# Chunks 0 to 5 of a gated linear attention: outputs as quadrant products, V in one transfer, and a new order of the work

## The chip, the cores and the metric

One core of a Trainium2 chip. The metric is device time in microseconds (us), the median of several executions. Engine names as in the profile: PE (TensorE matmuls) and PEld (its weight loads), DVE (VectorE), ACT (ScalarE), POOL (GpSimd), SP (SyncE, which issues nearly all DMAs).

## The reference

A gated linear attention and, on its output, a feed-forward network (FFN). Inputs q, k, v, alpha have shape (4, 8, 768, 48): batches, heads, steps, head size.

```python
for t in range(S):
    state = alpha[:, :, t, :, None] * state + np.einsum('bhd,bhe->bhde', k[:, :, t], v[:, :, t])
    y[:, :, t] = np.einsum('bhd,bhde->bhe', q[:, :, t], state)
...
x = attn_out.transpose(0, 2, 1, 3).reshape(B * S, H * D)      # 3072 x 384
h = x @ w_in                                                   # 384 x 2048
g = np.where(h >= 1, h, np.where(h <= -1, 0.0, (h + 1) ** 2 / 4))
return (g @ w_out).astype(np.float32)                          # 2048 x 384
```

The weights arrive as 64-bit floats and are decoded on the chip.

## The kernel before

**Chunks.** The 3072 steps are cut into 24 chunks of 128 (`CH`), six to a batch. Heads are taken in four pairs (`G`); a pair's two heads lie on partitions 0 to 47 and 64 to 111. For each chunk `prepare` loads a (alpha), k, q and v, and DVE runs two scans: products of alpha forwards into `Q` (L563), then backwards, inverted, into `inv` (L587). `Q` is multiplied by q (L613) and `inv` by k (L603). Early chunks get a, k or q with steps on the partitions (`tok_`), so PE first transposes them, four transposes to a tensor ("flips", L502); later ones get them laid by head dimension (`dim_`). Before, a and k are flipped for chunks 0 to 6 and q for chunks 0 and 1 (`EARLYQ`).

**Attention of a chunk** (`attend`, `follow`). A chunk has two halves of 64 steps. PE transposes the keys (L677), makes the scores of both halves (L690, 16 products in quadrants of the array), and the halves' updates of the state (L703). The scores are masked by DVE (L773) or, for one of the two heads in chunks 0 to 4, copied by ACT (L745) and masked by POOL (L755). The outputs (L827) are products over 128 partitions: one stationary tile `both` holds V on 64 partitions and the state on the other 64, and the moving tiles `Q` and `other` hold masked scores on one half and Q on the other. That needs copies: the state into `both` (L719, L720), half of `Q` into `other` (L737), and V twice, as `vt` and as `both` (L524, L535). The output goes to `ring` as a rounded part (ACT, L851) and its remainder (DVE, L856).

**FFN.** Three chunks form a group (`GROUP`), 16 column blocks f of w_in and w_out each. A group's block is 9 products with w_in (L924), the nonlinearity (ACT L953 twice, DVE L967, ACT L973, and a remainder by DVE or POOL, L974), and 9 products with w_out (L995). Groups 0 and 1 take blocks 0 to 7 first and 8 to 15 later, so that fewer weights are needed at the start. A block of group 0 with f = 0 is split by chunk (`SPLIT`), as 9 products of 128 columns. Two blocks share a weight unit u, each with a w_in and a w_out tile, decoded in six steps: ACT L380 and L388, DVE L396 and L407, POOL L420, ACT L433, then the remainder L435 on POOL or DVE.

**What sets the order.** Every operation is an entry with an engine, a duration and a due time (`key`), and `Plan.order` turns these into one fixed program order for each engine; engines and SP run their rows strictly in that order. Where the plan expects PE to wait over 0.45 us, and a PSUM bank is free, it puts in products of zeros (`fill`, L1084). Constants and tables at the file's top (`SHIFT`, `PREP`, `WFETCH`, ...) move due times of single chunks and weight units.

## Time and profile before

| | us |
|---|---|
| median of 3 runs | 505.77 (504.51 to 505.97) |
| profiled execution, its time | 505.32 |
| its span, first to last instruction | 503.6 |
| outside the span | 1.7 |
| PE busy in the span | 491.6 |
| DVE / ACT / POOL busy | 306.0 / 307.6 / 225.8 |

PE is busy for 98% of the span, but "busy" counts the products of zeros too, and the time of 4817 products is the sum over stages that differ: about 65 us in which chunks are prepared, weights are loaded and decoded and PE is partly filled, then some 430 us in which FFN products follow each other without a gap. Rows of the timeline carry: start, duration of the row's first to last instruction, engine, line, operation, tiles, shapes, count, and in brackets the idle time before and what ended it. An fp32 product of 64 rows or columns shows as two instructions.

### The profile page before, as it was taken

The page shows a single profiled execution, that of the slowest core. Times are in us where ns is not written, and L with a number is a line of the kernel's source. Part 1 is how long each engine was busy: PE and PEld are TensorE (multiplying, and loading weights), DVE is VectorE, ACT ScalarE, POOL GpSimd, SP SyncE. Part 2 cuts the span into 40 slices and gives each one's busy share as a digit, 9 for nine tenths or more (in the row PEclk, how much of TensorE's full clock was granted, in tenths as well). Part 3 has the DMA queues.
Part 4 walks back from the last instruction along what each step waited for, and adds up shares of the span by engine and source line. Part 5 has one row for each costly group of instructions (what it writes and reads, how often), then busy time and mean ns, then how long its engine had stood idle before and what let it go on. Part 6 is the DMA issues. An engine that isn't in the chain of part 4 may idle for free.

```text
span 503.6 us, 12167 instructions
## 1 busy us (share of the span) xinstructions
PE 491.6 (98%) x4817; PEld 475.4 (94%) x4817; DVE 306.0 (61%) x588; ACT 307.6 (61%) x599; POOL 225.8 (45%) x256
## 2 busy tenths in 40 slices
PE   7998999999999999999999999999999999999995
PEld 5887899999999999999999999999999999999995
DVE  6899988988957538866457457457457513121112
ACT  2689999968553656565555655556555655555551
POOL 4588564344245434545445534445355332333330
PEclk9999999999999999999999999999999999999998
DMA  8999978012345535455244443343213300000001
GB/s 226 358 262 321 351 246 235 9 53 64 112 112 166 147 75 134 116 156 153 51 113 113 115 105 107 74 117 101 65 34 62 90 0 13 14 17 31 1 1 51
DMA packets 61886, 57.56 MB, mean 114 GB/s; under 512 B 35745, under 2 KB 47617, under 8 KB 61825
## 3 DMA queue, kind: packets, MB, share of 16 engines
q1 hardware_dynamic: 61680, 56.64, 39.7%
q8 instruction: 39, 0.64, 0.5%
q14 instruction: 23, 0.18, 0.1%
q10 hardware_dynamic: 144, 0.10, 0.1%
HBM read 44.83 MB, written 9.83 MB: 109 GB/s over the span
## 4 chain that ended last, share of the span: by engine, by line
PE 89%; DMA 4%; DVE 2%; ACT 2%; SPq 1%; issue 1%; DVEq 0%
PE ps L924 40%; PE ps L995 39%; PE ps L827 5%; DMA raw<-in_laid_tok_k 2%; PE ps L703 2%; PE ps L690 2%; DMA vt<-in_laid_v 1%; PE ps L1084 1%; PE ps L502 1%; DMA ring<-ring 1%; SPq L485 1%; ACT gf L953 0%; PE ps L677 0%; SPq L872 0%; DVE Q L773 0%
## 5 line engine op out<-in xcount | busy, mean ns | idle before, releaser
L924 PE MATMUL ps<-ring,wt 128*128 128x384 f32 (+1 forms) x1170 | 223.6, 337 | 1.3 <-DMA ring<-ring 0.5
L995 PE MATMUL ps<-wt,gh 128*128 128x384 f32 x1152 | 222.5, 339 | 0.0
L924 PEld LDWEIGHTS ps<-ring,wt 128*128 128x128 f32 x1170 | 204.3, 188 | 2.4 <-DMA ring<-ring 0.9
L995 PEld LDWEIGHTS ps<-wt,gh 128*128 128x128 f32 x1152 | 201.2, 188 | 1.2
L974 POOL TENSOR_TENSOR gh<-gf,gh 128x384 fp32r<-128x384 f32 x101 | 108.9, 1080 | 171.0 <-ACT gh L973 167.8
L967 DVE SCALAR_TENSOR_TENSOR gf<-gf,ps 128x384 f32<-128x384 f32 x102 | 56.1, 550 | 149.7 <-ACT gf L953 148.4
L953 ACT ACTIVATE gf<-ps,half_b 128x384 f32<-128x384 f32 (+1 forms) x130 | 74.9, 577 | 92.7 <-PE ps L924 90.9
L973 ACT CAST gh<-gf 128x384 fp32r<-128x384 f32 x102 | 52.3, 513 | 63.0 <-DVE gf L967 63.0
L953 ACT ACTIVATE gf<-gf 128x384 f32<-128x384 f32 (+1 forms) x130 | 67.6, 520 | 3.9
L420 POOL TENSOR_TENSOR w<-w,wt 128x768 int32<-128x768 int32 x16 | 31.3, 1959 | 34.2 <-issue 7.7
L613 POOL TENSOR_TENSOR Q<-Q,raw 128x512 f32<-128x512 f32 x23 | 30.0, 1304 | 6.2 <-DVE bwd L567 3.8
L804 POOL TENSOR_TENSOR state<-state,last 128x192 f32<-128x192 f32 x20 | 18.6, 928 | 29.1 <-DVE state L729 28.1
L773 DVE TENSOR_TENSOR Q<-ps,mask 64x256 f32<-64x256 f32 x48 | 20.3, 422 | 15.1 <-ACT other L737 13.3
L827 PE MATMUL ps<-other,both 128*64 128x64 f32 x372 | 26.8, 225 | 0.0
L827 PE MATMUL ps<-Q,both 128*64 128x64 f32 x372 | 26.8, 225 | 0.0
L827 PEld LDWEIGHTS ps<-Q,both 128*64 128x64 f32 x372 | 23.5, 138 | 2.8 <-issue 1.3
L587 DVE TENSOR_TENSOR_SCAN inv<-raw,bwd 128x511 f32<-128x511 f32 x17 | 23.5, 1383 | 0.0
L827 PEld LDWEIGHTS ps<-other,both 128*64 128x64 f32 x372 | 23.5, 138 | 0.0
L563 DVE TENSOR_TENSOR_SCAN Q<-raw,fwd 128x512 f32<-128x512 f32 x17 | 20.7, 1219 | 0.2
L719 ACT COPY both<-state 48x192 f32<-48x192 f32 x49 | 17.1, 349 | 1.5 <-DVE state L727 0.5
L856 DVE TENSOR_TENSOR ring<-ps,ring 128x512 fp32r<-128x512 f32 (+1 forms) x24 | 16.1, 672 | 3.1 <-ACT ring L851 2.6
L703 PEld LDWEIGHTS ps<-vt,ks 64*64 64x64 f32 x352 | 13.4, 135 | 4.8 <-issue 3.5
(81 smaller groups left out, 473.9 us busy)
## 6 DMA issues: line engine op xcount, KB each, us to landing
both<-in_laid_v_both SPq DMA_DIRECT2D x48, 128.0 KB, 3.6
wt<-in_laid_w_in SPq DMA_DIRECT2D x8, 768.0 KB, 8.1
wt<-in_laid_w_out SPq DMA_DIRECT2D x8, 768.0 KB, 7.7
raw<-in_laid_dim_q SPq DMA_DIRECT2D x22, 256.0 KB, 2.8
out<-ot SPq DMA_DIRECT2D x23, 192.0 KB, 2.1
raw<-in_laid_dim_a SPq DMA_DIRECT2D x17, 256.0 KB, 2.9
raw<-in_laid_dim_k SPq DMA_DIRECT2D x17, 256.0 KB, 2.9
blocks<-part SPq DMA_DIRECT2D x15, 256.0 KB, 2.0
```

Of the source, the lines that this page charges most:

```text
L420: add = lambda e, c=c: e.tensor_tensor(out=bits()[:, c], in0=bits()[:, c], in1=word(I32, 0)[:, c], op=ALU.add)
L563: lambda: nc.vector.tensor_tensor_scan(flat(Q()), aT(), flat(fwd), 0.0, ALU.mult, ALU.max),
L587: lambda: nc.vector.tensor_tensor_scan(flat(inv())[:, 0:n][:, ::-1], aT()[:, 1 : n + 1][:, ::-1], flat(bwd)[:, 0:n][:, ::-1], bwd[:, G - 1 ...
L613: mul = lambda e: e.tensor_tensor(out=flat(Q()), in0=flat(Q()), in1=qT(), op=ALU.mult)
L703: nc.tensor.matmul(out=up(j, u)[64 * r : 64 * r + 64, g], lhsT=turnt[j]()[halves[u], g, 64 * r : 64 * r + 64], rhs=V[j]()[halves[u], g] if ...
L827: nc.tensor.matmul(out=ps()[halves[r], to, halves[u]], lhsT=lhsT[:, r, u], rhs=x()[:, g, halves[u]], start=m + u == 0, stop=True, skip_gro ...
L924: nc.tensor.matmul(out=h(), lhsT=win(f, w)[:, kt], rhs=ring[:, at, kt, a, :], start=(m == 0), stop=(m == 3 * KT - 1),)
L953: lambda: nc.scalar.activation(out=gf(), in_=in_(), func=func, scale=scale, bias=bias),
L967: lambda: nc.vector.scalar_tensor_tensor(out=x(), in0=gf(), scalar=1.0, in1=h(), op0=ALU.min, op1=ALU.max),
L973: plan.op("ACT", 0.08 + (0.45 if x is h else 0.41) * w, key + 0.4, lambda: nc.scalar.copy(out=gh()[:, 0], in_=x()), [x], [gh])
L974: sub = lambda e: e.tensor_tensor(out=gh()[:, 1], in0=x(), in1=gh()[:, 0].bitcast(F32), op=ALU.subtract)
L995: nc.tensor.matmul(out=o_ps[seg][t](), lhsT=gh()[:, a, (t - c0) * CH : (t - c0 + 1) * CH], rhs=wout(f, w), start=(f == f0 and i == 0), sto ...
```

## The change

Constants: `J0 = 6` makes chunks 0 to 5 (j < `J0`) take the new path; `EARLYQ` goes from 2 to 6 (q is flipped by PE for chunks 0 to 5); `KHELP = 2` and `QHELP = 2` let ACT copy k and q of chunks 0 and 1 out of PSUM and POOL multiply; `KPOOL = 9` gives POOL the multiplication by k of chunks 7 and 8; `ALONE` from 2 to 5 lets POOL or DVE, instead of DVE alone, take the remainder (L435) of units 2 to 4. The other constants and all tables of due times have new numbers, and the plan counts DMA time in packets.

For chunks 0 to 5:

- V arrives once, as one transfer of 192 KB (`tok_v`), in place of one of 96 KB and two of 128 KB.
- The outputs are separate products in quadrants: masked scores with V (64 rows) and Q with the state (48 rows). State and Q are no longer copied; the state before and after each half is kept in a ring of four tiles (`snap`), and the masked scores are one tile `other` of 128 partitions.
- The first part of the values' products ("crossed", r = 1 - u) stands ahead of the state's update on PE, the rest behind it.
- For each head one mask operation of 128 partitions takes the place of two of 64.

For later chunks `both` is packed, 48 columns to a head in place of 64, so V's two transfers are 96 KB each. The zeroing of `both` (L286) moves from the start to a place behind chunk 3's masks on POOL.

```diff
-EARLYQ = 2
+EARLYQ = 6
...
-ALONE = 2
+ALONE = 5
...
+J0 = 6
+SNAPS = 4
+NV = 2
+MEETN = 2
+KHELP = 2
+KPOOL = 9
...
+            if j < J0:
+                V[j] = lambda: vts[:, j % NV]
+                plan.op(
+                    "SP",
+                    Plan.ISSUE,
+                    key - LOAD + 1,
+                    lambda: nc.sync.dma_start(out=V[j]()[:, 0:DM], in_=laid["tok_v"][j]),
...
+            by_k = lambda e: e.tensor_tensor(out=flat(inv()), in0=flat(inv()), in1=kT(), op=ALU.mult)
+            if j < KHELP:
+                kq = buf("stage", "raw", [P, G * CH], 8)
+                plan.op("ACT", 0.55, key + 0.2, lambda kT=kT: nc.scalar.copy(out=kq(), in_=kT()), [kt], [kq])
+                kt, kT = kq, lambda: kq()
+            if EARLYK <= j < KPOOL or j < KHELP:
+                plan.op("POOL", 1.3, key, lambda: by_k(nc.gpsimd), [inv, kt], [inv], port=True)
...
+        def mask_apart(j, key):
+            S = others[j]
+            for r in range(2):
+                if j < (HELP if r else HELP0):
...
+                plan.op(
+                    "DVE",
+                    0.45,
+                    key,
+                    lambda r=r: nc.vector.tensor_tensor(
+                        out=S()[:, r], in0=ss(j, r), in1=mask[:, None].broadcast_to([P, G, HC]), op=ALU.mult
+                    ),
...
+        def rest_of(j, u, key, reads):
+            if group_of[j]:
+                return
...
+            plan.op("POOL", 0.3, key, lambda: nc.gpsimd.tensor_copy(out=to, in_=src()), reads, [name], port=True)
...
+        def outputs_apart(j, ps):
+            Q, S, n = prepared[j][0], others[j], group_of[j]
+            heads = [(g, g) for g in range(KT if n == 0 else G)]
...
+            def values(crossed):
+                ways = [(kt, KT, rest_v[:, :, kt]) for kt in range(KT) if n == 0] + [(g, g, None) for g, _ in heads]
+                for i, (to, g, v_) in enumerate(ways):
+                    for u in range(2):
+                        r = 1 - u if crossed else u
+                        lhsT = vs(j, u, r, g, wide) if v_ is None else v_[halves[u], r]
+                        put(to, r, u, lhsT, S()[halves[u], r, g], crossed and i == 0)
+
+            def states():
...
+                    for u in (1, 0)
+                    if snaps[j, u] is not None
+                    for to, g, s_ in ways
+                    for r in range(2)
...
+            def others_():
+                first_, *more = states()
+                first_()
+                values(False)
+                for x in more:
+                    x()
+            return lambda: values(True), others_
...
+                if j < J0:
+                    mask_apart(j, key)
+                    rest_of(j, None, key, [vt])
...
+                    crossed, rest = outputs_apart(j, lambda: ps())
+                    reads = [others[j], vt, *(["rest_v"] if n0 else [])]
+                    o = plan.op("PE", 0.05 + pair * (2 * KT if n0 else G), key, crossed, reads, [ps], mode="quad")
+                plan.op("PE", 0.55, key + 0.02, lambda: update(j), [ks, *v_of], meets[j], mode="quad", beside=True, after=[o])
+            if j < J0:
+                follow_apart(j, key)
+                us = 0.05 + pair * (2 * KT if n0 else G) * (3 if j % PER else 2)
+                plan.op("PE", us, key + 0.1, rest, [*used(j), *(["rest_v"] if n0 else [])], [ps], mode="quad")
+                end_chunk(j, ps, key + 0.1)
```

The numbers of PE's instructions in the whole program: products of zeros 105 before and 43 after, flips 64 and 80, output products 408 (L827) and 516 (288 at L1031, 228 at L909); key transposes, scores, updates and FFN products are as many as before.

How the order changes shows at three places. In after's program the flips are L528, the key transposes L738, the scores L751, the updates L771, the new products L909, FFN products L1146 and L1217.

**PE at chunk 0's attention.** Before, chunk 1's flips, then chunk 0's keys, scores and updates:

```order
L502 MATMUL ps<-ident,raw 128x128 x12
L677 MATMUL ps<-ident,inv 128x128 x4
L690 MATMUL ps<-Q,inv 64x64 x16
L703 MATMUL ps<-vt,ks 64x48
L703 MATMUL ps<-both,ks 64x48 x2
...
L502 MATMUL ps<-ident,raw 128x128 x8
```

After, from chunk 0's keys on:

```order
L738 MATMUL ps<-ident,inv 128x128 x4
L751 MATMUL ps<-Q,inv 64x64 x16
L528 MATMUL ps<-ident,raw 128x128 x12
L909 MATMUL ps<-other,both 64x64 x6
L909 MATMUL ps<-other,vt 48x64 x6
L771 MATMUL ps<-vt,ks 64x48 x16
L738 MATMUL ps<-ident,inv 128x128 x4
L751 MATMUL ps<-Q,inv 64x64 x16
L909 MATMUL ps<-Q,snap 48x64
```

Chunk 2's flips (all of a, k and q) and 12 crossed products now stand between chunk 0's scores and its updates, and chunk 1's keys and scores ahead of the rest of chunk 0's outputs.

**SP's transfers from chunk 2 on.** Before (tok_a, tok_k and dim_q are a, k and q; wt a weight tile):

```order
L485 DMA raw<-in_laid_tok_a 128x464
L485 DMA raw<-in_laid_tok_k 128x464
L485 DMA raw<-in_laid_dim_q 128x512
L535 DMA both<-in_laid_v_both 64x512 x2
L459 DMA wt<-in_laid_w_in 128x768
L524 DMA vt<-in_laid_v 128x192
L459 DMA wt<-in_laid_w_out 128x768
L485 DMA raw<-in_laid_tok_a 128x464
L485 DMA raw<-in_laid_tok_k 128x464
```

After, chunk 1's V, then chunk 2's a, k and q:

```order
L551 DMA vt<-in_laid_tok_v 128x384 x2
L511 DMA raw<-in_laid_tok_a 128x464
L511 DMA raw<-in_laid_tok_k 128x464
L511 DMA raw<-in_laid_tok_q 128x464
L485 DMA wt<-in_laid_w_in 128x768
L485 DMA wt<-in_laid_w_out 128x768
L485 DMA wt<-in_laid_w_in 128x768
L485 DMA wt<-in_laid_w_out 128x768
L511 DMA raw<-in_laid_tok_a 128x464
```

Ahead of chunk 3's a there were two weight tiles; now there are four.

**PE from chunk 6's keys to its scores.** Before, from chunk 6's keys (products of zeros, and chunk 5's outputs L827, are in the lines left out):

```order
L677 MATMUL ps<-ident,inv 128x128 x4
...
L924 MATMUL ps<-ring,wt 128x384 x9
...
L690 MATMUL ps<-Q,inv 64x64 x16
...
L924 MATMUL ps<-ring,wt 128x384 x18
```

After, the same stretch:

```order
L738 MATMUL ps<-ident,inv 128x128 x4
...
L909 MATMUL ps<-other,vt 64x64 x8
L771 MATMUL ps<-vt,ks 64x48 x8
L1146 MATMUL ps<-ring,wt 128x384 x9
L909 MATMUL ps<-Q,snap 48x64
L909 MATMUL ps<-other,vt 64x64 x8
L909 MATMUL ps<-Q,snap 48x64 x15
L1146 MATMUL ps<-ring,wt 128x384 x18
L751 MATMUL ps<-Q,inv 64x64 x16
```

Up to the end of chunk 6's scores and updates PE has 81 FFN products in its row before (63 at L924, 18 at L995) and 117 after (81 and 36); all attention of chunks 0 to 5 lies ahead of that point in both. From there on FFN products follow each other in both, broken only by the later chunks' bursts.

## Rows read from the trace of the kernel before

**Rows 1.** Stretches of 20 us: length, busy us by engine, granted clock, DMA share, GB/s
```profile
0.00:20.00 20.00, 16.59 (x256) 13.39 (x257) 14.84 (x33) 7.75 (x17) 9.33 (x24) 1.00 0.92 267
20.00:40.00 20.00, 19.46 (x356) 16.92 (x356) 18.54 (x42) 17.10 (x36) 16.45 (x21) 1.00 0.97 299
40.00:60.00 20.00, 18.29 (x263) 16.50 (x260) 19.05 (x43) 19.32 (x40) 13.11 (x13) 1.00 1.02 341
```

**Rows 2.** Timeline of PE: the FFN products behind chunk 6's scores and updates
```profile
62.13 3.40 PE L924 MATMUL ps<-ring,wt 128*128 128x384 f32 x18 [0.36 <-DVE ring L856]
```

**Rows 3.** Chain that ended last, by time: start, us, engine, line, count
```profile
33.75 1.96 PE ps L924 x18
...
114.36 3.14 PE ps L924 x18
```

**Rows 4.** Timeline of PE: products of zeros, at the start and later
```profile
1.06 3.38 PE L1084 MATMUL ps<-zeros 128*128 128x256 bf16 x15 [1.06 <-DVE zeros L259]
...
14.58 1.80 PE L1084 MATMUL ps<-zeros 128*128 128x256 bf16 x15
```

**Rows 5.** Timeline of PE: bursts of chunks 0, 1, 4
```profile
16.75 0.27 PE L827 MATMUL ps<-Q,both 128*64 128x64 f32 x1
...
18.29 0.70 PE L690 MATMUL ps<-Q,inv 48*64 48x64 f32 x32
...
21.55 1.19 PE L502 MATMUL ps<-ident,raw 128*128 128x128 f32 x8
22.67 0.27 PE L827 MATMUL ps<-Q,both 128*64 128x64 f32 x1
...
40.47 0.69 PE L690 MATMUL ps<-Q,inv 48*64 48x64 f32 x32
40.98 0.20 PE L703 MATMUL ps<-vt,ks 64*64 64x48 f32 x1
```

**Rows 6.** Timeline of DVE: preparation of chunk 1
```profile
9.40 0.16 DVE L553 TENSOR_SCALAR fwd<-ps 128x4 f32<-128x4 f32 x1
...
11.28 1.27 DVE L587 TENSOR_TENSOR_SCAN inv<-ps,bwd 128x511 f32<-128x511 f32 x1
...
14.53 0.18 DVE L599 RECIPROCAL meet<-inv 128x4 f32<-128x4 f32 x1
14.74 0.69 DVE L603 TENSOR_TENSOR inv<-inv,ps 128x512 f32<-128x512 f32 x1
15.35 0.68 DVE L613 TENSOR_TENSOR Q<-Q,ps 128x512 f32<-128x512 f32 x1
15.94 0.35 DVE L729 TENSOR_TENSOR state<-state,ps 128x192 f32<-128x192 f32 x1
```

**Rows 7.** Groups by line and shape, 0 to 80 us: busy us, mean ns, idle before
```profile
L407 DVE SCALAR_TENSOR_TENSOR w<-wt,w 128x768 int32<-128x768 int32 x8 | 7.7, 957 | 0.2
L773 DVE TENSOR_TENSOR Q<-ps,mask 64x256 f32<-64x256 f32 x14 | 5.9, 422 | 1.4 <-PE ps L703 0.7 <-ACT other L737 0.3
L967 DVE SCALAR_TENSOR_TENSOR ps<-gf,ps 128x384 f32<-128x384 f32 x9 | 5.0, 556 | 0.8 <-ACT gf L953 0.7
L396 DVE TENSOR_SCALAR w<-w 128x768 int32<-128x768 int32 x8 | 4.5, 559 | 0.0
L856 DVE TENSOR_TENSOR ring<-ps,ring 128x512 fp32r<-128x512 f32 x3 | 2.1, 689 | 0.6 <-ACT ring L851 0.6
```

**Rows 8.** DMA issues: count, KB each, median us to landing
```profile
both<-in_laid_v_both SPq DMA_DIRECT2D x48, 128.0 KB, 3.6
vt<-in_laid_v SPq DMA_DIRECT2D x24, 96.0 KB, 2.9
```

**Rows 9.** The end: PE's last products, and stretches behind them
```profile
495.13 3.04 PE L995 MATMUL ps<-wt,gh 128*128 128x384 f32 x16
...
500.50:501.00 0.50, 0.00 (x0) 0.00 (x0) 0.00 (x0) 0.00 (x0) 0.00 (x0) 0.83 0.16 49
501.00:502.00 1.00, 0.00 (x0) 0.00 (x0) 0.00 (x0) 0.00 (x0) 0.00 (x0) 0.50 0.03 8
```

More of the change, by code (lines that the diff above doesn't have):

```diff
@@ L148, in order @@
     def order(self):
-        free = {"PE": 1.0, "DVE": 1.0, "ACT": 1.0, "POOL": 4.6, "SP": 0.8}
+        free = {"PE": 1.0, "DVE": 1.0, "ACT": 1.0, "POOL": 2.6, "SP": 0.8}
         slots = {name: [(0.0, -i, None) for i in range(n)] for name, (n, share, _) in self.sizes.items() if share == name}
@@ L730, in grow @@
             plan.op("DVE", 0.33, key, make, [meets[j][u], "state"], ["state"])
+        snaps = {}
+        def mask_apart(j, key):
+            S = others[j]
+            for r in range(2):
+                if j < (HELP if r else HELP0):
+                    plan.op(
+                        "ACT", 0.39, key, lambda r=r: nc.scalar.copy(out=S()[:, r], in_=ss(j, r)), [meets[j][r]], [S], beside=r > 0
+                    )
+                    plan.op(
+                        "POOL",
+                        0.68,
+                        key,
+                        lambda r=r: nc.gpsimd.tensor_tensor(
+                            out=S()[:, r], in0=S()[:, r], in1=mask[:, None].broadcast_to([P, G, HC]), op=ALU.mult
+                        ),
+                        [],
+                        [S],
+                        port=True,
+                        beside=True,
+                        after=[plan.ops[-1]],
+                    )
+                    continue
+                plan.op(
+                    "DVE",
+                    0.45,
+                    key,
+                    lambda r=r: nc.vector.tensor_tensor(
+                        out=S()[:, r], in0=ss(j, r), in1=mask[:, None].broadcast_to([P, G, HC]), op=ALU.mult
+                    ),
+                    [meets[j][r]],
+                    [S],
+                    beside=r > 0,
+                )
@@ new lines, in follow_apart @@
+        def follow_apart(j, key):
+            last = prepared[j][2]
+            make = lambda: buf("att", "snap", [P, G, D], SNAPS)
+            if j % PER == 0:
+                snaps[j, 0] = None
+            old, mid = snaps[j, 0], make()
+            snaps[j, 1] = mid
+            if old is None:
+                plan.op("DVE", 0.3, key + 0.05, lambda: nc.vector.tensor_copy(out=mid(), in_=up(j, 0)), [meets[j][0]], [mid])
+            else:
+                plan.op(
+                    "DVE",
+                    0.33,
+                    key + 0.05,
+                    lambda: nc.vector.tensor_tensor(out=mid(), in0=old(), in1=up(j, 0), op=ALU.add),
+                    [meets[j][0], old],
+                    [mid],
+                )
+            rest_of(j, 1, key + 0.05, [mid])
+            if (j + 1) % PER == 0:
+                return
+            if j + 1 < J0:
+                new = snaps[j + 1, 0] = make()
+                at = lambda: new()
+            else:
+                new = "state"
+                at = lambda: state
+            plan.op(
+                "DVE",
+                0.33,
+                key + 0.2,
+                lambda: nc.vector.tensor_tensor(out=at(), in0=mid(), in1=up(j, 1), op=ALU.add),
+                [meets[j][1], mid],
+                [new],
+            )
+            decay = lambda e: e.tensor_tensor(
+                out=at(), in0=at(), in1=last()[:, :, None].broadcast_to([P, G, D]), op=ALU.mult
+            )
+            plan.op(
+                "POOL",
+                0.55,
+                key + 0.2,
+                lambda: decay(nc.gpsimd),
+                [new, last],
+                [new],
+                port=True,
+                other=("DVE", 0.36, lambda: decay(nc.vector), True),
+            )
+            if j + 1 < J0:
+                rest_of(j + 1, 0, key + 0.2, [new])
@@ L836, in used @@
         def used(j):
+            if j < J0:
+                rests = [("rest_s", j % 2, u) for u in range(2)] if group_of[j] == 0 else []
+                return [x for x in (prepared[j][0], others[j], ("vt", j % NV), snaps[j, 0], snaps[j, 1], *rests) if x is not None]
             i = j % NB
@@ L840, in used @@
                 + [(x, i, u, *r) for u in range(2) for x, r in (("v", ()), ("s", (0,)), ("s", (1,)))]
-                + [("rest", u) for u in range(2) if group_of[j] == 0]
             )
@@ L1095, in gated_attention_ffn @@
             due += SHIFT.get(j, 0.0)
+            if j == first[1]:
+                for r in range(2):
+                    plan.op(
+                        "POOL",
+                        0.8 * NB,
+                        due - 8.0,
+                        lambda r=r: nc.gpsimd.memset(both[HC * r : HC * (r + 1), :, r], 0.0),
+                        [],
+                        [*(("s", i, u, r) for i in range(NB) for u in range(2)), *(("rest_s", i, u) for i in range(2) for u in range(2)), "rest_v"],
+                        port=True,
+                    )
             prepare(j, due - PREPARE - PLACING * (j >= TURN) - PREP.get(j, 0.0))
```

278 lines of the change are left out of this document (166 added, 112 removed).

## The prediction

> **What bounds the kernel now.** I read the stretches of 20 us first [rows 1], to see where PE could be fuller. The granted clock is 1.00 throughout, PE is busy 54.3 of the first 60 us, and DVE 18.5 and 19.1 of 20 us in the second and third stretch. So two things hold in the front: PE looks full, but part of that is products of zeros, and DVE has no free time. Next I read the chain that ended last, by time [rows 3]: from about 62 us on it is FFN products alone, 18 in 3.14 us, or 0.174 us each. Nothing that happens behind that point can be shortened by this change, since FFN products, scores, updates and key transposes are as many as before. The question is how early PE gets through its front and how much of the FFN it has done by then. The mark is the end of chunk 6's scores and updates: before, PE is through with them at 61.8 us (62.13 less 0.36 of idle time, [rows 2]) with 81 FFN products done. The change's order has 117 done at the same mark. The 36 more are worth 36 x 0.174 = 6.3 us. The 0.36 us of idle time and two products of zeros that follow the mark before come to 0.6 us. So the changed kernel is level if it reaches the mark at 61.8 + 6.3 + 0.6 = **68.7 us**; each us earlier is a us gained.
>
> **PE's own work up to the mark.** Output products: before, 24 in 1.54 us (16.75 to 18.29, [rows 5]), 64 ns each, since products of 128 rows and 64 columns run two at a time, one in each half of the columns. After, 228 products in quadrants stand in place of 120. No row shows just this pattern. The nearest rows are the L827 burst (two at a time) and the scores, 16 in 0.51 us (40.47 to 40.98, [rows 5]), 32 ns each, whose order goes round all four quadrants. In the new functions two quadrants on a diagonal alternate, so I take the pace of two at a time without the burst's ends, 58 ns: 228 x 0.058 = 13.3 us against 120 x 0.064 = 7.7, so 5.6 us more. The bounds are 7.3 us (four at a time, 0.4 less than before) and about 26 us (one at a time, which the scores' pace speaks against). Flips: 8 in 1.12 us (21.55 to 22.67, [rows 5]), 0.14 each, 16 more of them, 2.2 us. With the 6.3 us of FFN products PE gets 14.1 us more useful work ahead of the mark. What it loses is products of zeros: 60 fewer ahead of the mark, 15 in 1.80 us [rows 4], 7.2 us. If PE's real waits stayed as they are (5.7 us idle in 60 us, [rows 1], 1.1 of them at the start [rows 4]) the mark would come at 61.8 + 14.1 - 7.2 = 68.7 us: exactly level. If all of those waits but the start's went, it would come at 64.1 us, 4.6 us sooner. That is the most that can be gained.
>
> **DVE's queue up to the mark.** The second way to the same number follows DVE, because chunk 6's keys need its last scan. A chunk's preparation takes 3.15 us for both scans and their small operations (9.40 to 12.55, [rows 6]), 0.21 for the reciprocal and 0.61 for the product with k, 3.97 in all, and 0.6 more where Q is multiplied by DVE. The change takes some work from DVE: one mask of 0.42 us [rows 7] for each chunk, and for chunks 0 and 1 the reciprocal and the product with k, 1.6 us together, which POOL does. It gives DVE the products with q of chunks 2 to 5, which POOL did, 4 x 0.6 = 2.4 us, less that of chunk 1. So DVE's load is nearly the same, and the copies that go away were ACT's and POOL's. From chunk 3's first operation to chunk 6's last product with k, DVE's row holds four preparations (15.9), three products with q (1.8), nine decode steps at 0.56 and 0.96 (6.6, [rows 7]), six state sums of 0.3 (1.8, the slot behind 15.94, [rows 6]), two masks (0.9), and four ring remainders and twelve FFN operations, half of them on one chunk only (6.8, from 0.69 and 0.56 for the full ones, [rows 7]): 33.8 us.
>
> When does chunk 3 start? Its a now stands behind four weight tiles instead of two: 5.9 MB with its own 232 KB. At the 267 and 299 GB/s of the first two stretches [rows 1] that is 19.8 to 22.1 us; I take 21.7, since the later transfers of a stretch are seldom early, and its flips are done at 22.3. V as one transfer of 192 KB in place of 96 and twice 128 [rows 8] is what keeps this from being later: three chunks' worth, 0.5 MB, 1.7 us. Then PE's row runs: the rest of chunk 1 (36 x 0.058 = 2.1), 8 flips (1.1), two times 9 small FFN products (2 x 0.98, [rows 3]), chunk 2's crossed products (0.7), keys, updates and scores (1.7), the rest of chunk 2 (2.1), and some 0.8 us for POOL's copies of the state's leftover columns, which stand in POOL's row behind decode steps. Chunk 2's output is done at about 32.7, and with 1.1 us for ACT, which has decode work ahead of its copy, DVE can take the remainder at 33.9. It reaches that row at 31.0, so it waits 2.9 us; chunk 4's scans are queued behind this wait (before, they stood ahead of chunk 2's remainder). DVE is through with chunk 6's keys at 22.3 + 33.8 + 2.9 = 59.0. Behind that PE still has the key transposes (0.6), chunk 5's crossed products behind two masks (0.9), half an update (0.3), 27 FFN products (4.7), 24 output products (1.4), and scores and updates (1.1): 9.0 us. The mark comes at **68.0 us**, 0.7 before level.
>
> Edits that I cost at nothing: POOL's later zeroing of `both`, which lies ahead of a stretch in which POOL waits for DVE's decode; without that cover it costs PE nothing before chunk 6's V arrives. The fewer copies on ACT and POOL are off PE's path now, since the decode of w_in for f = 2 is done some 8 us ahead of its product; they are worth something only if ACT or POOL turn out to be late. The new numbers for chunks 7 and later move rows behind the mark, where a burst is ready long before its turn.
>
> **Sum.** The profiled execution took 505.32 us (span 503.6 and 1.7 outside), 0.45 under the median of 505.77. 505.3 - 0.7 = **504.6 us** against the profiled one, which is what I give; against the median the same sum gives 505.1. A difference below 0.3%, 1.5 us, can't be told from no change here.
>
> **Rivals.**
>
> *Faster: the quadrants overlap as four.* The values' products and the state's stand next to each other and use other rows, so the engine may run more than two at a time. At the scores' 32 ns [rows 5] the new products cost 7.3 us. Chunk 2's rest is then 0.9 us shorter ahead of DVE's wait, the last 32 products 0.8, and chunk 1's rest no longer holds up chunk 3's flips: the mark comes at 66.0, and the time is 502.6. For it speaks the scores' row, against it that a burst of the new code keeps to one diagonal. The Trainium skill, TensorEngine Tiling (Array Packing), section Tiling Modes, says that 64 x 64 tiles are four that work independently; by that rule this rival is the end to expect, and the scores' row agrees with the rule, but no row shows a diagonal. Chance 0.2.
>
> *Slower: chunk 3's a lands late.* Its flips stand on PE ahead of chunk 1's rest, and DVE has nothing else than chunk 3's scans in its row, so each us of delay is a us at the mark. It decides from a landing at 22.4 us on. If the start of the run moves at the 267 GB/s and its first 2 us move nothing, 24.1 us is possible: 2.4 us later, 507.0. PE's waits for a, k and q in the front are the kind that it would join. Chance 0.2.
>
> *Slower: the clock falls.* With fewer products of zeros PE can idle longer. After the last product of the run, at 498.2, the granted clock is 1.00 to 500.5 and 0.50 from 501 on [rows 9], so 2.3 us of idleness did not lower it and 2.9 did. The first 15 products of zeros took 3.38 us, the same number later 1.80 [rows 4]: a fall costs about 1.6 us. The longest wait of PE in my walk is about 1 us, so it would take a mistake of 1.5 us in one place. The time would be 506.2 plus that wait, 507.7. The Trainium skill, TensorE: Matmul & The Clock Gate, section HAM oscillation, says that waits of PE for DMA between bursts make the gate fall back to the half rate each time; that speaks against removing the products of zeros, and no row before the end shows it. Chance 0.05.
>
> **How the numbers follow.** The walk by DVE's queue holds with chance 0.55, 504.6, itself between 502.9 and 506.3 (waits of PE 1.7 us fewer or more): faster 0.20, same 0.32, slower 0.03. Four quadrants 0.2, all faster. Late a 0.2: slower 0.17, same 0.03. Clock 0.05, slower. That makes faster 0.40, same 0.35, slower 0.25. The range reaches from 501.8 (four quadrants and 0.8 us fewer waits) to 507.4 (late a with its own spread); it leaves out the full 4.6 us and the fallen clock.
>
> **What would show each step.** In the profile of the changed kernel: 24 output products of a chunk in 1.4 us (L909, two at a time) or 0.8; chunk 3's flips at 22 us; the ring remainder of chunk 2 (L1062) near 34 us with a wait for ACT or PE before it; the end of chunk 6's scores and updates at 68 us, with products of zeros no longer seen behind 60 us; DVE's busy share of 20 to 60 us still above 0.9. The prediction is wrong if PE waits over 1 us in one place between 35 and 68 us, or if FFN products with w_out wait for a decoded tile, which I take to be ready in time.

## The result: slower by 1.4%, and the profile after

The changed kernel takes **512.85 us** (median of 4 runs, 510.63 to 513.34), the kernel before 505.19 beside it: ratio 1.0141, 95% interval 1.0122 to 1.0160. The forecast was 504.6, with a range up to 507.4. The profiled execution took 513.34 us, span 511.6, against 505.32 and 503.6.

The stretches that answer to [rows 1] (the same columns), and below them three that frame the loss:

```profile
0.00:20.00 20.00, 16.97 (x311) 14.35 (x313) 15.46 (x34) 10.34 (x19) 10.16 (x28) 1.00 0.91 340
20.00:40.00 20.00, 16.98 (x329) 15.55 (x322) 12.95 (x30) 11.80 (x25) 13.01 (x16) 0.90 0.95 365
40.00:60.00 20.00, 20.00 (x308) 18.45 (x308) 16.64 (x37) 14.61 (x26) 12.94 (x11) 0.93 0.77 269
30.00:33.00 3.00, 3.00 (x98) 2.87 (x91) 1.34 (x4) 1.81 (x5) 2.68 (x4) 1.00 1.06 424
33.00:36.00 3.00, 1.33 (x40) 1.12 (x36) 0.59 (x2) 1.07 (x3) 1.49 (x2) 0.99 1.00 386
36.00:42.50 6.50, 6.50 (x27) 6.22 (x27) 3.69 (x8) 3.73 (x7) 2.33 (x3) 0.50 0.65 211
```

DVE, 18.5 of 20 us busy in the second stretch before, has fallen to 13.0. From 33 to 36 us every engine is idle half the time or more while the DMA engines are full. From 36.0 to 42.5 PE is "busy" all the time with 27 matmuls, at a granted clock of 0.50. What PE waited for over the whole run, the longest three (us in total, times, longest us):

```profile
PE ps L909 <- issue: 3.4, 3, 1.7
PE ps L738 <- POOL inv L656: 1.4, 2, 1.1
PE ps L771 <- DMA ks<-blocks: 1.1, 1, 1.1
```

The first row is new: 3.4 us in three waits for which the profile knows no releaser. Before, such waits came to 0.2 us:

```profile
PE ps L703 <- issue: 0.2, 1, 0.2
```

The second of the three rows is small beside the 3.4 us for a, k and q before, which are gone; the third lies behind the mark, at 230 us. PE's timeline around them, and at the mark:

```profile
17.44 0.37 PE L909 MATMUL ps<-Q,snap 48*48 48x64 f32 x6 [0.48 <-issue]
...
21.49 0.60 PE L528 MATMUL ps<-ident,raw 128*128 128x128 f32 x4
...
23.60 0.51 PE L909 MATMUL ps<-other,both 64*64 64x64 f32 x11 [1.27 <-issue]
...
33.57 0.39 PE L909 MATMUL ps<-Q,both 48*64 48x64 f32 x7
35.63 0.38 PE L909 MATMUL ps<-Q,both 48*64 48x64 f32 x5 [1.67 <-issue]
...
37.35 1.52 PE L1146 MATMUL ps<-ring,wt 128*128 128x128 f32 x6
...
45.16 0.25 PE L909 MATMUL ps<-Q,snap 48*48 48x64 f32 x1
...
46.45 0.27 PE L751 MATMUL ps<-Q,inv 48*64 48x64 f32 x2
...
73.43 1.83 PE L1146 MATMUL ps<-ring,wt 128*128 128x384 f32 x9
```

The last row answers to [rows 2]: the mark came at 73.4 us, not at 68.0, with the 117 FFN products done that the order gives it. Level was 68.7. So 4.7 of the 8.0 us of span are lost ahead of the mark. Behind it PE waits 1.3 us more than before (the 1.1 us for `ks` is one of these), the stretch after PE's last product is 1.3 us longer, and the rest, 0.7, is by how much the 36 FFN products and the two of zeros were worth less than the 6.9 us reckoned. The DVE row that waits for chunk 2's output, by its timeline:

```profile
36.56 0.56 DVE L1062 TENSOR_TENSOR ring<-ps,ring 128x384 fp32r<-128x384 f32 x1 [2.17 <-ACT ring L1057]
```

The 1.67 us wait is hardly one for data: it splits chunk 2's products of state and Q, all with the same operands, with 7 matmuls of one kind ahead of it and 5 behind. Counting all of PE's instructions in the trace from the start (weight loads, matmuls and its semaphore instructions), 449, 705 and 1217 stand ahead of the three waits: once and twice 256 apart. At 961, which lies between the last two, PE paused 0.3 us. The page lists a DMA queue that moves instructions, q8: 41 packets and 0.67 MB, 16 KB each, for PE's some 10,000 instructions (4987 loads and as many matmuls), so some 250 to a packet; before, it was 39. Here is what the DMA engines of the changed kernel moved from 29.7 us, where PE passed number 961, and from 33.3 us on (queue and kind: packets, MB, share of 16 engines):

```profile
q1 hardware_dynamic: 538, 1.50, 104.3%
q14 instruction: 1, 0.01, 0.5%
...
q1 hardware_dynamic: 66, 0.40, 97.7%
q8 instruction: 1, 0.02, 5.8%
```

For 3.6 us after PE passed into the new 256, q1 alone filled the engines, with weights and chunks; then the next packet of q8 ran, 33.31 to 34.24, and 1.4 us behind its end PE went on. It is the same at each of the three: the packet starts 3.0 to 3.7 us after PE entered its last 256 instructions, takes 0.9 to 1.1, and PE resumes 1.4 to 1.5 us later. While the engines are full, PE gets 256 instructions in about 6.1 us (17.44, 23.60, 29.71, 35.63). An output product is four instructions, two loads and two matmuls, in 54 ns, and there are 228 where 120 were.

### The profile page after: what moved, and what is told of

Read it like the earlier page. It is cut to its first block, busy times and chain, and to the rows that moved or that the text cites. A ratio compares the mean times of both kernels' runs of the same rounds, so it can differ in the third digit from the quotient of the medians.

```text
span 511.6 us, 12486 instructions
## 1 busy us (share of the span) xinstructions
PE 496.8 (97%) x4987; PEld 480.9 (94%) x4987; DVE 297.7 (58%) x578; ACT 301.7 (59%) x587; POOL 231.2 (45%) x247
## 4 chain that ended last, share of the span: by engine, by line
PE 84%; DVE 8%; POOL 2%; issue 2%; DMA 1%; ACT 1%; SPq 0%; DVEq 0%; POOLq 0%; ACTq 0%
PE ps L1146 36%; PE ps L1217 36%; PE ps L1031 4%; PE ps L771 2%; PE ps L751 2%; PE ps L909 2%; DVE Q L601 1%; DVE inv L625 1%; PE ps L1306 1%; PE ps L528 1%; POOL wt L461 1%; DVE w L433 1%; POOL w L446 1%; DVE wt L461 1%; DMA blocks<-part 1%
## 5 line engine op out<-in xcount | busy, mean ns | idle before, releaser
L1146 PE MATMUL ps<-ring,wt 128*128 128x384 f32 (+1 forms) x1170 | 226.2, 339 | 0.2 <-DMA ring<-ring 0.2
L1217 PE MATMUL ps<-wt,gh 128*128 128x384 f32 x1152 | 221.8, 339 | 0.3 <-POOL wt L461 0.3
L1146 PEld LDWEIGHTS ps<-ring,wt 128*128 128x128 f32 x1170 | 206.2, 190 | 1.3 <-issue 0.5
L1217 PEld LDWEIGHTS ps<-wt,gh 128*128 128x128 f32 x1152 | 201.4, 188 | 1.8 <-POOL wt L461 0.6
L670 POOL TENSOR_TENSOR Q<-Q,raw 128x512 f32<-128x512 f32 x20 | 25.9, 1297 | 10.4 <-DVE inv L617 7.2
L1008 POOL TENSOR_TENSOR state<-state,last 128x192 f32<-128x192 f32 x15 | 13.7, 916 | 27.8 <-DVE state L797 27.8
L461 POOL TENSOR_TENSOR wt<-w,wt 128x768 fp32r<-128x768 f32 x10 | 19.8, 1985 | 4.6 <-ACT wt L459 4.4
L1057 ACT CAST ring<-ps 128x512 fp32r<-128x512 f32 (+1 forms) x24 | 13.8, 573 | 12.8 <-PE ps L1031 6.3
L1031 PE MATMUL ps<-other,both 128*64 128x64 f32 x288 | 20.6, 225 | 0.0
L1031 PE MATMUL ps<-Q,both 128*64 128x64 f32 x288 | 20.6, 225 | 0.0
L610 POOL TENSOR_SCALAR last<-Q 128x4 f32<-128x4 f32 x24 | 7.8, 323 | 27.5 <-DVE Q L601 24.4
L991 DVE TENSOR_TENSOR Q<-ps,mask 64x256 f32<-64x256 f32 x36 | 15.2, 423 | 7.9 <-ACT other L952 7.1
L1031 PEld LDWEIGHTS ps<-Q,both 128*64 128x64 f32 x288 | 18.1, 138 | 1.4 <-issue 0.3
```

Source lines behind the costliest of these rows:

```text
L461: sub = lambda e, c=c: e.tensor_tensor(out=part(1)[:, c], in0=data()[:, c], in1=part(0).bitcast(F32)[:, c], op=ALU.subtract)
L670: mul = lambda e: e.tensor_tensor(out=flat(Q()), in0=flat(Q()), in1=qT(), op=ALU.mult)
L1031: nc.tensor.matmul(out=ps()[64 * r : 64 * r + w.shape[1], to, halves[u]], lhsT=w, rhs=x()[:, g, halves[u]], start=m + u == 0, stop=True, s ...
L1146: nc.tensor.matmul(out=h(), lhsT=win(f, w)[:, kt], rhs=ring[:, at, kt, a, :], start=(m == 0), stop=(m == 3 * KT - 1),)
L1217: nc.tensor.matmul(out=o_ps[seg][t](), lhsT=gh()[:, a, (t - c0) * CH : (t - c0 + 1) * CH], rhs=wout(f, w), start=(f == f0 and i == 0), sto ...
```

## Experiments

**Is it instructions or data?** `shift` puts 64 cheap instructions at PE's start, so that every later place moves 64 in the count.

```diff
             for _ in range(n):
                 nc.tensor.matmul(out=idle, lhsT=zeros, rhs=nothing, start=True, stop=True)
+            for _ in range(32 if n == WARM else 0):
+                nc.tensor.matmul(out=idle[:, 0:2], lhsT=zeros, rhs=zeros[:, 0:2], start=True, stop=True)
```

> The changed kernel with 32 products of zeros of 2 columns put behind the 15 products of zeros at PE's very start: 64 more instructions (a weight load and a matmul each), early, where PE still waits for data; nothing else moves. Theory A: PE's three unexplained waits (0.48 us at 17.44, 1.27 at 23.60, 1.67 at 35.63) are waits for the next 256 of its instructions, which reach the chip in transfers of 16 KB. Then the waits come 64 instructions, 32 matmuls, earlier in the program: of the products of chunk 2's outputs between 31.9 and 36.0, where now about 75 matmuls stand ahead of the 1.67 us and 5 behind, 40 to 48 stand ahead and 33 to 40 behind. Rival B: the wait is one for data or for a buffer (the copies of rest_s and rest_v): it stays where it is, with 5 matmuls behind it. Time by either: within 2 us of the changed kernel (510.6 to 513.3).

Measured: 510.45 us, just under the range expected, ratio to before 1.0124 (1.0095 to 1.0153). PE's timeline where the second wait stands now:

```profile
20.73 0.47 PE L751 MATMUL ps<-Q,inv 48*64 48x64 f32 x14
23.40 0.46 PE L751 MATMUL ps<-Q,inv 48*64 48x64 f32 x16 [2.21 <-issue]
```

The wait left the outputs of chunk 1 and stands in the middle of chunk 2's scores, 64 instructions earlier in the program: again with 705 instructions ahead of it, and at 23.4 us, where it was at 23.6. That excludes data and buffers for this wait. The forecast for the third wait could not be seen: the longer second wait lowered the clock (0.52 from 24.0 to 27.5), PE came late to the next place, and found its instructions there.

**The same from the other side.** `thin` leaves out 12 products of chunk 2 (state times Q of its first half), 48 instructions.

```diff
-                for x in more:
+                for x in more[: 11 if j == 2 else None]:
                     x()
```

> The changed kernel without the last 12 of chunk 2's products of state and Q (those of its first 64 rows are left out, so that chunk's outputs lack them): 48 of PE's instructions and, at 58 ns a product, 0.7 us of its work. Theory A: the place where PE must have the next 256 instructions moves from 10 instructions ahead of the end of chunk 2's products to some 38 behind it, past the transposes and zeros and into the FFN products, which PE reaches when the instructions are there. So the 1.67 us wait goes altogether (under 0.3 us), and with it the fall of the clock: 0.7 us less work brings chunk 2's end 2.2 to 2.6 us forward, the FFN products of 37.7 to 42.5 take 2.6 us, the end of chunk 6's scores and updates is 4 to 5 us earlier (68.5 to 69.5), and the time 507 to 509.5. Rival B (a wait for data or a copy): the wait stays in front of chunk 2's last products, and the time falls by 0.7 us at most, to 511.5 to 513.

Measured: 507.12 us, ratio 1.0028 (1.0010 to 1.0047). PE's waits, and the stretches that were half idle and at half clock:

```profile
PE ps L909 <- issue: 1.3, 1, 1.3
```

```profile
33.00:36.00 3.00, 2.60 (x21) 2.14 (x19) 2.15 (x6) 2.93 (x7) 2.94 (x4) 1.00 1.02 405
36.00:42.50 6.50, 6.50 (x154) 6.01 (x153) 6.19 (x15) 5.53 (x12) 1.55 (x4) 1.00 0.81 288
```

The wait at 35.6 is gone and so is the fall: 154 matmuls in 36.0 to 42.5 where there were 27. The mark is at 68.3. So 0.7 us less work brought the mark forward by 5.1 us and the time by 5.7.

**What is the clock's part?** `hold` fills the wait with products of zeros, which change no result (`HELD = {2: 11}`).

```diff
                 first_()
                 values(False)
-                for x in more:
+                for x in more[:4]:
+                    x()
+                for _ in range(HELD.get(j, 0)):
+                    nc.tensor.matmul(out=ps()[:, 0:KT], lhsT=zeros, rhs=padding, start=False, stop=True, skip_group_check=True)
+                for x in more[4:]:
                     x()
```

> The changed kernel with 11 products of zeros of 384 columns (estimate: 0.16 us each at full clock, from 0.11 us for 256 columns, so 1.8 us) accumulated into chunk 2's output bank in the middle of its burst of products, ahead of the 1.67 us wait; zeros added change no result, nothing else moves. Theory A (the wait is for instructions, and the idle time is what made the granted clock fall to 0.50 from 36.0 to 42.5): PE is busy while the instructions come, the wait shrinks below 0.5 us, the clock stays at 1.00 through 36 to 43, the 18 FFN products of 37.7 to 42.5 take 2.6 us instead of 4.8, the end of chunk 6's scores and updates comes 2 to 3.5 us earlier than 73.4, and the time is 509.0 to 511.0. Rival B (the clock falls for another reason, or its fall costs nothing at the end): the clock falls all the same, or the time stays at 512 to 513.5.

Measured: 508.84 us, just under the range expected, ratio 1.0089 (1.0059 to 1.0119). Its stretch and its timeline:

```profile
36.00:42.50 6.50, 6.28 (x90) 5.68 (x88) 5.43 (x13) 5.52 (x11) 2.33 (x3) 1.00 0.71 227
```

```profile
32.80 1.63 PE L947 MATMUL ps<-zeros 128*128 128x384 bf16 x9
...
35.40 0.32 PE L911 MATMUL ps<-Q,snap 48*48 48x64 f32 x4 [0.16 <-issue]
35.55 0.52 PE L911 MATMUL ps<-Q,both 48*64 48x64 f32 x12
```

The instructions come when they came (35.4 against 35.6), but the clock stays at 1.00, and the mark is at 70.8. So the idling from 34.0 to 35.6 made the clock fall, since nothing else differs here, and the fall is worth 2.6 us at the mark. The edit also answers for the third wait what `shift` could not: it puts 22 instructions ahead of the pause, and the pause stands 11 matmuls earlier (16 behind it in place of 5), again with 1217 instructions ahead. The profiled executions differ by 4.6 us (513.34 and 508.71); 2.1 of these lie behind the last product, where that stretch is shorter, which other runs do not bear out as the edit's (below).

**What makes the instructions late?** `defer` moves three weight units (4.6 MB) out of the stretch: their transfers (`fetched`) go behind chunk 6's keys in SP's row, and ACT's step that scales them in place (`lowered`, L414) next to ACT's first decoding step (`scaled`, L406). PE's row is untouched.

```diff
+LATE = (2, 3, 4)
...
+            at = loaded["k", 6]
+            for u in LATE:
+                for x, which in (("w_in", "i"), ("w_out", "o")):
+                    move(fetched[u, x], at)
+                    at = fetched[u, x]
+                    move(lowered[u, which], scaled[u, which])
```

> The changed kernel with the transfers of the weight tiles 2, 3 and 4 (six of 768 KB, 4.6 MB) moved in SP's row from 19 to 27 us to behind chunk 6's keys (33.3 us), and the ACT step that scales these tiles in place moved next to their decoding, since it would wait for them; PE's row is the same word for word. Theory A1 (the next 256 instructions come late because their transfer stands behind the weights'): in the stretch from 22 to 36 us the distance between such transfers falls from 6.1 us to under 5, the 1.67 us wait is under 0.6, the clock holds 1.00, chunk 2's outputs are done 1 to 3 us before 36.0 and the time is 506 to 510.5. Rival A2 (they come late whatever the DMA engines carry): the waits stay at 6.1 us of distance and the time is within 1 us of the changed kernel, 512 to 514. Later weights may make an FFN product wait for a decoded tile: then a wait of PE on POOL wt shows after 50 us.

Measured: 511.91 us, ratio 1.0152 (1.0119 to 1.0185). Stretches, PE's timeline and waits:

```profile
24.00:33.00 9.00, 9.00 (x235) 8.49 (x231) 6.05 (x13) 4.76 (x11) 5.57 (x8) 1.00 0.29 80
36.00:42.50 6.50, 6.50 (x154) 6.00 (x153) 6.22 (x14) 3.62 (x9) 1.74 (x4) 1.00 0.98 372
56.00:59.50 3.50, 3.18 (x12) 2.84 (x13) 3.39 (x8) 1.94 (x3) 3.19 (x3) 0.51 1.01 423
```

```profile
34.49 0.77 PE L1148 MATMUL ps<-ring,wt 128*128 128x128 f32 x5 [0.19 <-DVE ring L1064]
```

```profile
PE ps L530 <- DVE gh L1198: 1.6, 1, 1.6
PE ps L911 <- issue: 1.5, 2, 1.3
PE ps L530 <- DVE ring L1064: 1.4, 1, 1.4
```

The packet that PE asked for at 23.2 us shows in the stretch from 24.2 to 24.4:

```profile
q8 instruction: 1, 0.02, 33.5%
```

With the engines at 0.29 it starts after 1.1 us instead of 3.6, the third wait is gone, PE never idles from 24 to 33 us, and the FFN products start at 34.0 instead of 37.4. So the instructions come late where weights are queued ahead of their packet. The time did not follow and fits neither of the two ranges: the moved weights delayed unit 5's, for whose scaling ACT stood 3.7 and 2.3 us; PE waited 1.6 and 1.4 us for DVE, which waited for ACT, and the clock fell again (0.51 from 56.0 to 59.5). In `late` (below), where ACT does not stand for unit 5, these two waits are gone.

**Is the clock held by products of zeros before, too?** `bare` takes 60 of the 90 later ones from the kernel before, as many as the change takes ahead of the mark. Its condition also spares every row of 15, so beside the first 15 two more rows stay, which the expectation overlooked:

```profile
15.70 2.06 PE L1084 MATMUL ps<-zeros 128*128 128x256 bf16 x15
41.02 1.80 PE L1084 MATMUL ps<-zeros 128*128 128x256 bf16 x15
```

```diff
-            for _ in range(n):
+            for _ in range(n if n == WARM else 0):
                 nc.tensor.matmul(out=idle, lhsT=zeros, rhs=nothing, start=True, stop=True)
```

> The kernel before without its products of zeros behind the first 15 (some 88 matmuls between 5 and 66 us); nothing else moves. It is one part of the change alone. Theory: PE has these only where it waits anyway, so what they do is hold the granted clock: without them PE idles over 1 us at several places between 14 and 40 us, the clock falls to 0.50 in some of these stretches, and the time is 1 to 4 us longer, 506.5 to 509.5; fewer instructions ahead also make the next 256 come earlier, so no unexplained wait over 0.3 us. Rival (they are worth nothing, as the prediction took for the 60 that the change removes): 504.5 to 506.

Measured: 506.60 us, ratio 1.0034 (1.0018 to 1.0051).

```profile
9.00:16.50 7.50, 7.08 (x90) 6.08 (x90) 5.67 (x13) 2.48 (x6) 2.39 (x5) 0.54 1.06 270
29.50:37.00 7.50, 6.23 (x65) 5.78 (x66) 6.26 (x14) 4.98 (x10) 7.33 (x8) 0.54 0.93 278
```

The clock fell twice, behind a wait of 1.5 us and during one of 2.8, each time for 6.8 us. The whole edit cost about 2 us, less than the 2 x 3.4 that half the clock could cost in these stretches; why it is less is not shown. So these 60 products of zeros are worth about 2 us there, not nothing.

**What is the change worth without these waits?** The next seven runs move the changed kernel's weight transfers and ACT's scaling steps as `defer` does, by other tables. `spread` puts each unit behind the chunk's tensor that the table names, just ahead of its decoding; `spread1` does not move unit 1.

```diff
+LATE = {1: ("k", 5), 2: ("a", 6), 3: ("k", 6), 4: ("q", 6)}
```

> The changed kernel with the transfers of weight tiles 1 to 4 moved back in SP's row to where their decoding comes soon: tile 1 behind chunk 5's keys, tile 2 behind chunk 6's a, tile 3 behind chunk 6's keys, tile 4 behind chunk 6's queries; ACT's step that scales these tiles (and tiles 5 to 7) in place stands next to their decoding. PE's row is the same. In defer the DMA engines carried nothing from 30 to 33 us and then 4.6 MB in a row, for which ACT waited 3.7 and 2.3 us; here they should carry the weights evenly. Theory A1 (the instructions' transfers are late while the DMA engines carry weights and chunks at once): the distance of these transfers falls below 5 us also between 15 and 24 us, the 0.48 and 1.27 us waits fall below 0.2 and 0.6, the third is gone, the clock is 1.00 throughout, the end of chunk 6's scores and updates is at 66.5 to 69.5 us, and the time is 504 to 507.5. Rival (a queue that waits for a late weight tile takes what PE gains, as in defer): PE waits over 1 us for DVE or ACT between 36 and 70 us, and the time is 508.5 to 512.

> As spread, but weight tile 1 stays where it is (issued at 7.6 and 8.2 us): tiles 2 to 4 alone are moved. Theory A1: up to 24 us the row is as in the changed kernel, so the waits of 0.3 to 0.5 us at 17 and 1.27 us at 23 stay; the third (1.67) is below 0.4, the clock holds 1.00, the end of chunk 6's scores and updates is 1.0 to 1.8 us later than in spread, and the time 505 to 509. Rival as for spread: a wait for a late weight tile over 1 us, 508.5 to 512.

Measured: 515.39 us, ratio 1.0171 (1.0119 to 1.0222), and 515.04, ratio 1.0176 (1.0145 to 1.0208). Both times lie above the theory's range and the rival's. PE's timeline in `spread`:

```profile
34.49 0.38 PE L912 MATMUL ps<-Q,both 48*64 48x64 f32 x5 [2.22 <-issue]
```

With unit 2 issued at 24.8 us, the packet asked for at 28.0 waited 4.0 us. So it is not enough to carry the weights more evenly: with a unit queued when PE enters a new 256, the packet comes as late as in the changed kernel. The wait at 23 us did go in `spread`, where unit 1 had moved. Scaling beside decoding cost 3.4 us more at 112 us, as in the next two. `late1`, and `late` without the table's first entry, keep the engines free of weights from some 25 to 32 us:

```diff
+LATE = [(("k", 5), (1,)), (("k", 6), (2,)), (("a", 7), (3,)), (("q", 7), (4, 5)), (("k", 9), (6, 7))]
```

> As defer, with what defer did wrong mended: weight tile 2 behind chunk 6's keys, tile 3 behind chunk 7's a, tiles 4 and 5 behind chunk 7's queries, tiles 6 and 7 behind chunk 9's keys, and ACT's scaling step of tiles 2 to 7 next to their decoding, so that ACT's row waits for none of them. In spread and spread1 the instructions asked for at 28 us came 3.7 to 4 us late because weight tile 2 was on the engines then; here, as in defer, nothing but chunks is on them from 24 to 32 us. Theory A1: third wait under 0.4 us, clock 1.00 through 30 to 60, waits of 17 and 23 us as in the changed kernel (0.3 to 0.5 and 1.27), no wait over 0.6 us between 36 and 70 us, end of chunk 6's scores and updates at 67.5 to 70, time 504.5 to 508. Rival: the waits of 1.6 and 1.4 us that defer showed at 54 and 56 us stay, so they were not for ACT's scaling of tile 5; time 509 to 513.

> As late, with weight tile 1 behind chunk 5's keys as well (as in spread), and its scaling step next to its decoding. Theory A1: the instructions asked for at 17 us come after 1.4 us instead of 3.7, the 1.27 us wait at 23 us is gone, what remains is at most 0.3 us at 17 and 0.5 us near 28; chunk 2's outputs are done 1 to 1.5 us before late's; if DVE does not bind first, the end of chunk 6's scores and updates is at 66.5 to 69 and the time 503.5 to 507. Rival (DVE's row binds from chunk 2's outputs on): no more than 0.4 us is left of this at the end, and the time is late's.

Measured: 512.16 us, ratio 1.0126 (1.0091 to 1.0162), and 510.49, ratio 1.0106 (1.0061 to 1.0151). The fronts are as expected, marks at 68.1 and 67.1; the times are not, for one wait of PE, in `late1` from 103.5 us on, with the clock at 0.50 from 106.4 to 109.8:

```profile
PE ps L1220 <- ACT gh L1198: 3.4, 1, 3.4
```

ACT's copy of hidden values stands there behind decoding with its scaling beside it. The last three use `late1`'s transfers and put the scaling steps into places that other units' steps have in the changed kernel (below `last3`'s table, place and steps, i for w_in and o for w_out; in `last` and `last2` unit 2's two go to (4, 'o'), (3, 'i') and to (3, 'o'), (5, 'i'), and the others follow).

```diff
+SWAP = {(2, 'i'): [(1, 'o')], (3, 'i'): [(2, 'i')], (3, 'o'): [(2, 'o')], (5, 'i'): [(3, 'i')], (5, 'o'): [(3, 'o')], (6, 'i'): [(4, 'i')], (6, 'o'): [(4, 'o')], (7, 'i'): [(5, 'i')], (7, 'o'): [(5, 'o'), (6, 'i')]}
```

> As late1, but ACT's scaling steps of tiles 1 to 7 stand, where that can be, in the places that other tiles' steps have in the changed kernel, two to four places later than now, instead of next to their decoding. In late and late1 PE waited 3.4 us at 103 us for ACT's copy of hidden values, behind the decoding of tiles 4 and 6 with its scaling beside it, and the granted clock then fell to 0.50 (0.66 over 105 to 110); by late1's own rows that is 3.4 + 2.6 us of its last product's end at 503.8. Theory: the front stays as late1's (end of chunk 6's scores and updates at 67.2, no unexplained wait over 0.6 us), the 3.4 us wait and that fall are gone, the last product ends at 497.5 to 499.5, and the time is 503 to 506, beside 504.5 to 506 for the kernel before. Rival: the scaling steps in their new places wait for late tiles, PE waits over 1 us between 36 and 110 us, time 507 to 511.

> As last, with the scaling steps of tiles 2 to 4 in later places again (in last ACT waited 3.0 us at 38 to 41 us for tile 2, and PE waited 2.4 us at 41.1 for the masks behind that step, after which the granted clock fell to 0.79 and 0.87 over 40 to 50), and those of tile 6 in the places of tile 7's. Theory: front as late1's, end of chunk 6's scores and updates 67.0 to 67.6, neither the 2.4 us wait of last nor the 3.4 us wait of late1, clock 1.00 up to the end, last product's end 497 to 498.5, time 502.5 to 505. That is what the change is worth without its waits for instructions: level with the kernel before or up to 0.5% faster. Rival: a third place where ACT or POOL waits for a late tile, over 1 us of PE between 36 and 120 us, and 506 to 509.

> As last, with the scaling steps of tiles 2 to 5 one place later (tile 2's two where tile 3's are in the changed kernel, 45.7 and 47.6 us), tile 6's first step behind tile 5's second. In last ACT stood 3.0 us for tile 2 and PE 2.4 us for the masks behind it, and the clock fell for 10 us after; in last2 the steps were two to three places later and PE waited 1.3 us at 66 for POOL's decoding and 1.1 us at 105. Theory: neither of these; end of chunk 6's scores and updates 67.0 to 67.6, the clock 1.00 to the end, last product 497 to 499, time 502.5 to 505.5, level with the kernel before or up to 0.5% faster. Rival: ACT or POOL again stands for a late tile, over 1 us of PE between 36 and 120 us, and 506 to 510.

Measured: `last` 507.80 us, ratio 1.0046 (1.0029 to 1.0063); ACT stood 3.0 us for unit 2, PE 2.4 behind it. `last2` 510.49, ratio 1.0118 (1.0093 to 1.0144); PE waited 1.3 us for POOL's decoding and 1.1 for ACT, the mechanism of its rival, but the time lies above the rival's range too. `last3` **505.64, ratio 1.0016 (0.9999 to 1.0034)**, just above the range expected, with the mark at 67.1 and no wait of PE over 1 us behind the start; its profiled execution was its fastest, 503.93. What is left of its waits for instructions, and its stretches against [rows 1]:

```profile
PE ps L914 <- issue: 0.3, 1, 0.3
```

```profile
0.00:20.00 20.00, 17.36 (x330) 14.47 (x331) 15.74 (x35) 10.52 (x19) 10.15 (x29) 1.00 0.88 309
20.00:40.00 20.00, 19.73 (x439) 18.17 (x435) 16.17 (x38) 12.91 (x27) 13.67 (x17) 1.00 0.73 249
40.00:60.00 20.00, 19.73 (x280) 17.69 (x272) 19.24 (x41) 15.11 (x26) 17.42 (x14) 1.00 1.03 396
```

PE has 439 matmuls in the second stretch, where the changed kernel had 329. So with the instructions there in time the changed kernel is level with the kernel before. That is the worth of the change and of the moved transfers and scaling steps together; the kernel before was not given such moves. No version beat the kernel before.

## Why the prediction was wrong, step by step

- **Pace of the output products: right.** 24 products of chunk 3 from 45.16 to 46.45 us, 54 ns each, for 58 forecast. That is the pace of two at a time, and the faster rival is out. The Trainium skill, TensorEngine Tiling (Array Packing), section Tiling Modes, lets four 64 x 64 tiles work independently; this order of products, which alternates between the two tiles of a diagonal, does not get there.
- **Chunk 3's a: right.** Its flips were done at 22.1 us, forecast 22.3. That slower rival did not occur.
- **The walk from there: right as far as it counted work.** With the instructions in time (`last3`) DVE's last product of chunk 6's keys released PE at 57.3 us, forecast 59.0, and the mark came at 67.1, forecast 68.0. But level was set too late: that mark is 1.6 us ahead of the 68.7, and PE's last product still ended only 0.3 us earlier than before (497.87 against 498.18 us). Behind the mark, where the prediction took everything as unchanged, PE waits 0.8 us more than before, and the 36 FFN products and the two of zeros were worth 0.5 us less than the 6.9 reckoned.
- **The step that failed: "the longest wait of PE in my walk is about 1 us."** The walk priced products by their duration alone, 0.058 us, and had no term for the instructions that they are. The three waits are 3.4 us, and 1.67 stood in one place, ahead of DVE's ring remainder of chunk 2 (forecast 33.9, started 36.56 after a wait of 2.17). "DVE's busy share of 20 to 60 us above 0.9" became 0.65 and 0.83. The one trace of this before was a wait of 0.19 us without releaser at 19.18, with 451 instructions ahead of it, and I took no notice of it: PE went on behind numbers 449 and 705 at 19.07 and 25.28 us, 6.2 us apart, after pauses of 0.3 and 0.2 us and 1.3 to 1.4 us behind the ends of its packets. The kernel before already stood at that limit there.
- **The clock: right mechanism, wrong chance and size.** It was the rival with chance 0.05, and it is what happened. The price of 1.6 us plus the wait was the term mis-sized: `hold` puts the fall alone at 2.6 us, since the clock stood at 0.50 for 6.8 us (35.96 to 42.79) and PE had flips and FFN products to do: 18 of these took from 37.35 to 42.30 us, in `hold` from 36.74 to 39.83. The price had been read from the first 15 products of zeros, ahead of 5.9 us, where the profile's record of the clock begins; the 1.00 in [rows 1] says nothing of them. The reason given for the small chance, that 2.3 us of idleness at the end did not lower the clock [rows 9], did not carry over to the middle. The Trainium skill, TensorE: Matmul & The Clock Gate, section HAM oscillation, says that waits between bursts make the gate fall back each time, a rule that I set aside. The trace agrees for the wait of 1.67 us; behind those of 0.48 and 1.27 us the clock stayed at 1.00.
- **The sum.** The mark missed the forecast by 5.4 us. Counted from `last3`, whose mark at 67.1 holds 0.3 us of waits for instructions, the 3.4 us of these waits and the 2.6 of the clock make 72.8, so 0.6 of the way to 73.4 stays open. The 1.3 us longer stretch behind the last product stays open: with the same row on PE it was 4.3 us in `last3`, 4.4 in `defer`, 6.6 in `spread` and 6.7 in the changed kernel, so nothing here ties it to the change.

## What to carry to other kernels

Where an engine's row turns into more and shorter instructions, count them: reckon the time of each stretch also as instructions over the pace at which they arrive, and look at the trace for waits without a releaser, however short, since they show that limit before it bites. Keep large transfers from being queued when a dense stretch begins. Products of zeros that hold the clock are a cost that also buys something, and what they buy is read only from a stretch in which PE waits.

## What the runs showed of the hardware

- PE's instructions arrive by DMA, 256 at a time (449, 705, 961 and 1217 stood ahead of its pauses), one packet ahead. With weights queued the packet started 3.0 to 4.1 us after PE entered the previous 256; with the engines nearly idle, 1.0 to 1.1 us (`defer` at 23.2, `late1` at 28.0). The copy takes 0.9 to 1.1, and PE went on 1.2 to 1.6 us after its end wherever it waited. The Trainium skill, Runtime: NRT & Kernel Launch, section Instruction fetch mechanics, has the blocks of 16 KiB or 256 instructions and the engine's own DMA queue for them, and the trace agrees; it calls the crossing mostly hidden, and here it was not, at 0.5, 1.3 and 1.7 us.
- What PE did ahead of a fall of the granted clock to 0.50: single waits of 1.67, 2.2, 2.3, 2.4, 2.8 and 3.4 us, one of 1.46, and 1.56 with 1.40 close behind. No fall followed waits of 1.0 to 1.27 us, in over ten places, nor one of 1.51 in `hold` at 227 us. The falls came between 0.9 us ahead of the end of these waits and 1.8 us behind it, and the low stretches lasted 3.4 or 6.8 us.
